# A DeltaNet layer followed by a gated feed-forward block: the same work in another hand-written order

## The chip, the cores and the metric

The kernel runs on one core of a Trainium2 chip, in one launch. The metric is the device time of that launch in microseconds (us). Before the change three runs took 638.85, 640.1 and 642.2 us; their median is 640.1 us.

A core has five engines, each with an instruction queue of its own that it works through strictly in order: PE (TensorE, matrix products), DVE (VectorE), ACT (ScalarE), POOL (GpSimd) and SP (SyncE, which only issues transfers). An instruction whose inputs are not there stops its engine's queue until they come. Transfers (DMAs) are issued here from SP's and ACT's queues, and seven at the start from POOL's.

## The reference

```python
def _attn_ref(q, k, v, beta):               # (4, 8, 768, 48), beta (4, 8, 768)
    k_n = k / (np.linalg.norm(k, axis=-1, keepdims=True) + 1e-06)
    state = np.zeros((B, H, D, D))
    for t in range(S):
        kt, vt, bt = (k_n[:, :, t], v[:, :, t], beta[:, :, t, None])
        y[:, :, t] = np.einsum('bhd,bhde->bhe', q[:, :, t], state)
        v_old = np.einsum('bhde,bhd->bhe', state, kt)
        state = state + bt[:, :, :, None] * np.einsum('bhd,bhe->bhde', kt, vt - v_old)
    return y

def _moe_ref(x, w_in, w_out):               # x (3072, 384), w_in (384, 2048), w_out (2048, 384)
    h = x @ w_in
    g = h * np.cos(h)
    return g @ w_out
# x = the attention's y, transposed to (batch, time, heads * head_dim)
```

All data are float32.

## The kernel before, in words

**The attention** is worked in 24 units n of 32 time steps. Each unit holds all four batches and eight heads. For each unit: `turn` and `turn_out` transpose keys and queries (from unit 6 on, `blocks` loads and DVE transposes do this); `gram` multiplies them on PE, `gram_keys` and `gram_queries` scale and mask the products on DVE. The triangular matrix of a unit must be inverted. For units 0 and 1 this is done by repeated doubling: `double(n, level, half)` on PE (L759) and its `double_copy` (ACT), `double_turn` and `double_add` (DVE), six levels in a chain. From unit 2 on it is done for pairs m = (2m, 2m+1) column by column on POOL: `gram_put` writes the matrices to DRAM, `gram_get` reads them back in another layout, `inv(m, 0..6)` (L879 and L886; `inv(1, 0)` on DVE) eliminates, `put` writes the result, `get` reads it back for one unit. `eye` fills the start value.

Then comes the **recurrence**, which runs from unit to unit: `state(n)` (PE, L930) multiplies by the state, `right(n)` (DVE, L947) forms the right side, `solve(n)` (PE, L1002) multiplies by the inverse, `solve_out(n)` (DVE, L1014) scales, `update(n)` (PE, L1027) and `update_out(n)` (DVE, L1035 or L1037) make the next state. For units 2 and 3 the solve has two halves: `solve_half`, `half_out` (ACT), `between`, `between_out` (DVE), `solve` (L960, L996). Off this chain, `within`, `within_out` (ACT), `features` (PE, L1078) and `features_out` (ACT) make the feed-forward block's input.

**The feed-forward block** takes units in pairs p, 256 tokens. Pair 0 is worked plainly: eight `hidden(0, f)` (PE, L1099, 12 products each), the gate h·cos h by `turns`, `cos` (ACT), `rest`, `gate` (DVE), and eight `out(0, i, k)` (PE, L1297). From pair 1 on both products are Strassen-like: sums of inputs `x_sum` (POOL or DVE, L1188), `layer(p, x)` (PE, L1273), `layer_out` (ACT or DVE), then `left`, `right` sums, `out(p, step, part)` (PE, L1355), `collect` and `store`. `in_sums` and `right` make the sums of the weights. The weights come in 28 pieces by `weights(t)`, are brought to another form by `split(t)` (ACT, L528, L532), `shift(t)` (DVE, L536) and `add(t)` (POOL, L540), and use the same eight tiles as the gates and the squares of the keys (`square`), so that a `weights(t)` or a `square` can wait for the `add` that empties its tile.

**The order** is written out by hand. `Order.add` records 2,199 pieces, each with its dependencies. `Order.LINE` is a list of their numbers; `run` emits the pieces in that order, and each engine then works through its own pieces in that order. Buffers are given out in this order too, first freed first taken. `Order.OTHER` names the pieces that go the other way where there are two: transfers go to ACT's queue if they are named there and to SP's otherwise, sums go to POOL or DVE. `warm(i)` pieces are matmuls on an unused bank (L495) that fill PE's idle time; they emit nothing once the first `out` has been emitted. The last loop of the kernel pins the instructions of each engine in the emitted order.

```python
line = [keys[int(i)] for i in self.LINE.split()]
for key in line:
    emit, deps, makes, uses = self.tasks[key]
    assert deps <= done, key
    for tag, t in makes:
        self.place[t] = free[tag].pop(0)
    emit()
```

Of the kernel before, what the change touches and what calls it, by code (L numbers as in the profile page):

```python
# [59 lines left out]
class Order:  # L60

    OTHER = {
        ('v', 0), ('v', 1), ('gram_put', 2), ('gram_put', 3), ('inv', 1, 0), ('put', 1),
        ('gram_put', 4), ('v', 5), ('gram_get', 2), ('put', 2), ('gram_put', 6), ('v', 8),
        ('v', 9), ('blocks', 9, 0), ('blocks', 9, 1), ('put', 4), ('get', 10), ('v', 11),
        ('blocks', 11, 0), ('blocks', 11, 1), ('gram_put', 11), ('gram_get', 5), ('v', 12),
        ('gram_put', 13), ('gram_get', 6), ('get', 13), ('v', 14), ('blocks', 14, 0), ('v', 15),
        ('blocks', 15, 0), ('blocks', 15, 1), ('v', 16), ('gram_put', 16), ('v', 17), ('k', 18),
        ('v', 18), ('get', 18), ('v', 20), ('gram_put', 21), ('gram_get', 11), ('store', 0, 1),
        ('right', 4, 4), ('left', 1, 1, 0), ('left', 1, 3, 0), ('left', 1, 3, 1),  # L70
        ('store', 1, 0), ('store', 1, 1), ('x_sum', 2, 'd'), ('x_sum', 2, 'n'),
        ('x_sum', 2, 'm'), ('x_sum', 2, 'e'), ('x_sum', 2, 'k'), ('x_sum', 2, 'g'),
        ('x_sum', 2, 'i'), ('x_sum', 2, 'l'), ('x_sum', 2, 'f'), ('x_sum', 2, 'b0'),
        ('left', 2, 4, 1), ('left', 2, 3, 1), ('x_sum', 3, 'd'), ('x_sum', 3, 'n'),
        ('x_sum', 3, 'm'), ('x_sum', 3, 'e'), ('x_sum', 3, 'k'), ('x_sum', 3, 'g'),
        ('x_sum', 3, 'i'), ('x_sum', 3, 'l'), ('x_sum', 3, 'h'), ('x_sum', 3, 'b0'),
        ('left', 3, 4, 1), ('left', 3, 3, 1), ('store', 3, 0), ('store', 3, 1),
        ('x_sum', 4, 'd'), ('x_sum', 4, 'm'), ('x_sum', 4, 'g'), ('x_sum', 4, 'i'),
        ('left', 4, 3, 0), ('left', 4, 3, 1), ('x_sum', 5, 'd'), ('x_sum', 5, 'e'),
        ('x_sum', 5, 'l'), ('x_sum', 5, 'h'), ('x_sum', 5, 'b0'), ('left', 5, 2, 0),  # L80
        ('left', 5, 4, 1), ('left', 5, 3, 0), ('left', 5, 3, 1), ('x_sum', 6, 'd'),
        ('x_sum', 6, 'g'), ('x_sum', 6, 'l'), ('x_sum', 6, 'f'), ('x_sum', 6, 'b0'),
        ('left', 6, 1, 0), ('left', 6, 4, 0), ('store', 6, 0), ('x_sum', 7, 'd'),
        ('x_sum', 7, 'm'), ('x_sum', 7, 'g'), ('x_sum', 7, 'i'), ('x_sum', 7, 'f'),
        ('x_sum', 7, 'h'), ('x_sum', 7, 'b0'), ('left', 7, 4, 0), ('left', 7, 4, 1),
        ('left', 7, 3, 1), ('store', 7, 0), ('x_sum', 8, 'd'), ('x_sum', 8, 'm'),
        ('x_sum', 8, 'e'), ('x_sum', 8, 'k'), ('x_sum', 8, 'g'), ('x_sum', 8, 'l'),
        ('left', 8, 3, 0), ('store', 8, 0), ('store', 8, 1), ('x_sum', 9, 'd'),
        ('x_sum', 9, 'm'), ('x_sum', 9, 'e'), ('x_sum', 9, 'k'), ('x_sum', 9, 'i'),
        ('x_sum', 9, 'l'), ('x_sum', 9, 'b0'), ('left', 9, 1, 0), ('left', 9, 2, 0),  # L90
        ('left', 9, 1, 1), ('left', 9, 3, 0), ('store', 9, 1), ('x_sum', 10, 'k'),
        ('x_sum', 10, 'i'), ('x_sum', 10, 'l'), ('x_sum', 10, 'h'), ('x_sum', 10, 'b0'),
        ('left', 10, 1, 0), ('left', 10, 1, 1), ('left', 10, 4, 1), ('left', 10, 3, 0),
        ('left', 10, 3, 1), ('store', 10, 1), ('x_sum', 11, 'd'), ('x_sum', 11, 'e'),
        ('x_sum', 11, 'k'), ('x_sum', 11, 'g'), ('x_sum', 11, 'f'), ('left', 11, 1, 0),
        ('left', 11, 2, 0), ('left', 11, 1, 1), ('left', 11, 3, 0), ('left', 11, 3, 1),
        ('store', 11, 1), ('store_right', 11), ('weights', 2), ('weights', 3), ('weights', 4),
        ('weights', 9), ('weights', 11), ('weights', 12), ('weights', 13), ('weights', 14),
        ('weights', 15), ('weights', 17), ('weights', 23), ('weights', 24)
# [1849 lines left out]
```

## Time and profile before

| | |
|---|---|
| median of three runs | 640.1 us |
| profiled execution | 642.77 us |
| its span, first to last instruction | 641.0 us |
| granted TensorE clock, mean | 0.98 |
| busy: PE, DVE, POOL, ACT | 612.1, 504.4, 435.1, 297.5 us |
| chain that ended last: PE, DMA, POOL, DVE | 76%, 8%, 5%, 5% |

Busy time is time in which an engine has at least one instruction in it. The chain that ended last is found by going back from the last instruction, each time to what released it. In a row of the order of time, "x24" counts matmul records: a float32 product is two records, a transpose one.

### The profile page before, as it was taken

The page shows a single profiled execution, that of the slowest core. Times are in us where ns is not written, and L with a number is a line of the kernel's source. Part 1 is how long each engine was busy: PE and PEld are TensorE (multiplying, and loading weights), DVE is VectorE, ACT ScalarE, POOL GpSimd, SP SyncE. Part 2 cuts the span into 40 slices and gives each one's busy share as a digit, 9 for nine tenths or more (in the row PEclk, how much of TensorE's full clock was granted, in tenths as well). Part 3 has the DMA queues.
Part 4 walks back from the last instruction along what each step waited for, and adds up shares of the span by engine and source line. Part 5 has one row for each costly group of instructions (what it writes and reads, how often), then busy time and mean ns, then how long its engine had stood idle before and what let it go on. Part 6 is the DMA issues. An engine that isn't in the chain of part 4 may idle for free.

```text
span 641.0 us, 24058 instructions
## 1 busy us (share of the span) xinstructions
PE 612.1 (95%) x10096; PEld 571.4 (89%) x10096; DVE 504.4 (79%) x1051; ACT 297.5 (46%) x533; POOL 435.1 (68%) x791
## 2 busy tenths in 40 slices
PE   6978788999999999999999999999999999999997
PEld 4857777788799998999999999999999999999997
DVE  5876736999999897788878788978878676757872
ACT  3546535645543543543743553643544443635440
POOL 4428877788888888786886786888884881212231
PEclk8897979999999999999999999999999999999999
DMA  9876656655354645446234445333225011000001
GB/s 187 218 169 174 136 130 134 148 87 83 72 87 74 103 74 96 69 67 111 42 52 87 75 79 91 54 45 70 45 35 101 18 31 23 20 3 15 13 20 30
DMA packets 215844, 50.75 MB, mean 79 GB/s; under 512 B 207384, under 2 KB 210744, under 8 KB 215736
## 3 DMA queue, kind: packets, MB, share of 16 engines
q1 hardware_dynamic: 161132, 32.34, 27.8%
q10 hardware_dynamic: 54300, 16.33, 12.1%
q8 instruction: 79, 1.29, 0.8%
q0 software_dynamic: 304, 0.54, 0.4%
q14 instruction: 29, 0.24, 0.1%
HBM read 38.95 MB, written 10.22 MB: 77 GB/s over the span
## 4 chain that ended last, share of the span: by engine, by line
PE 76%; DMA 8%; POOL 5%; DVE 5%; issue 2%; SPq 2%; ACT 1%; ACTq 1%; DVEq 0%; POOLq 0%
PE p_out L1355 30%; PE p_h L1273 28%; PE p_kq L930 3%; PE p_s L1027 3%; POOL part L879 2%; POOL z L886 2%; PE p_u L1002 2%; PE p_kq L1057 2%; PE p_g L675 2%; PE p_h L1099 2%; DMA qp<-in_q_dram 2%; PE p_h L1355 2%; DMA kp<-in_k_dram 2%; PE p_z L1078 1%; DMA w_sum<-z_dr 1%
## 5 line engine op out<-in xcount | busy, mean ns | idle before, releaser
L879 POOL TENSOR_TENSOR part<-z,gb 128x126 f32<-128x126 f32 (+23 forms) x321 | 141.6, 441 | 44.1 <-DMA gb<-g_dr 17.5
L886 POOL TENSOR_TENSOR z<-z,part 128x126 f32<-128x126 f32 (+23 forms) x321 | 142.8, 445 | 25.2
L1355 PE MATMUL p_out<-w_out,g_ffn 128*128 128x192 f32 x672 | 121.0, 329 | 0.0
L1355 PEld LDWEIGHTS p_out<-w_out,g_ffn 128*128 128x128 f32 x672 | 107.9, 190 | 1.0
L1152 ACT ACTIVATE turns<-turns,halfpi 128x512 f32<-128x512 f32 x96 | 68.0, 718 | 83.2 <-DVE turns L1143 71.6
L1273 PE MATMUL p_h<-x_sum,w_in 128*128 128x128 f32 x704 | 92.3, 278 | 0.0
L1355 PE MATMUL p_out<-w_sum,g_ffn 128*128 128x192 f32 x496 | 88.7, 328 | 0.0
L1273 PEld LDWEIGHTS p_h<-x_sum,w_in 128*128 128x128 f32 x704 | 85.6, 191 | 1.9
L1136 ACT ACTIVATE turns<-g_ffn,quarter_turn 128x512 int32<-128x512 f32 x77 | 55.0, 719 | 66.3 <-DVE g_ffn L1155 35.4
L1355 PEld LDWEIGHTS p_out<-w_sum,g_ffn 128*128 128x128 f32 x496 | 79.6, 190 | 0.6
L1290 DVE TENSOR_TENSOR g_ffn<-g_ffn,p_h 128x512 f32<-128x512 f32 x88 | 59.5, 679 | 14.7 <-PE p_h L1273 13.7
L1155 DVE TENSOR_TENSOR g_ffn<-turns,g_ffn 128x512 f32<-128x512 f32 x77 | 61.7, 810 | 11.7 <-ACT turns L1152 11.6
L1143 DVE SCALAR_TENSOR_TENSOR turns<-g_ffn,turns 128x512 f32<-128x512 f32 x77 | 57.1, 750 | 8.2 <-ACT turns L1136 8.1
L1273 PE MATMUL p_h<-x_sum,in_sum 128*128 128x128 f32 x440 | 58.9, 278 | 0.8 <-POOL x_sum L1188 0.8
L1273 PEld LDWEIGHTS p_h<-x_sum,in_sum 128*128 128x128 f32 x440 | 54.3, 191 | 2.2 <-POOL x_sum L1188 1.0
L1070 ACT COPY y<-p_kq 32x384 f32<-32x384 f32 x96 | 45.1, 470 | 19.0 <-PE p_kq L1057 8.1
L1407 DVE SCALAR_TENSOR_TENSOR o<-p_out,o 128x192 f32<-128x192 f32 x74 | 25.1, 351 | 29.7 <-PE p_out L1355 29.5
L1273 PE MATMUL p_h<-x_ffn,w_in 128*128 128x128 f32 x352 | 46.6, 277 | 1.0 <-ACT p_h L1285 1.0
L1273 PEld LDWEIGHTS p_h<-x_ffn,w_in 128*128 128x128 f32 x352 | 43.0, 192 | 1.6 <-ACT p_h L1285 1.3
L574 POOL TENSOR_TENSOR knrm<-ksum,halves 128x16 f32<-128x16 f32 (+1 forms) x14 | 37.1, 2647 | 10.1 <-DVE ksum L562 9.5
L1371 POOL TENSOR_TENSOR g_ffn<-g_ffn 128x512 f32<-128x512 f32 x15 | 19.1, 1271 | 30.5 <-DVE g_ffn L1155 26.6
L1285 ACT COPY p_h<-p_h 128x512 f32<-128x512 f32 x44 | 25.3, 575 | 28.5 <-PE p_h L1273 20.4
(168 smaller groups left out, 1051.7 us busy)
## 6 DMA issues: line engine op xcount, KB each, us to landing
g_ffn<-in_moe_w_in_dram SPq DMA_DIRECT2D x7, 512.0 KB, 7.8
g_ffn<-in_moe_w_out_dram SPq DMA_DIRECT2D x9, 384.0 KB
kp<-in_k_dram SPq DMA_DIRECT2D x136, 24.0 KB, 2.5
gb<-g_dr SPq DMA_DIRECT2D x12, 256.0 KB, 3.9
g_ffn<-in_moe_w_out_dram ACTq DMA_DIRECT2D x7, 384.0 KB
g_ffn<-in_moe_w_in_dram ACTq DMA_DIRECT2D x5, 512.0 KB, 5.9
vp<-in_v_dram ACTq DMA_DIRECT2D x52, 48.0 KB, 2.7
zt<-z_dr SPq DMA_DIRECT2D x68, 32.0 KB, 2.7
```

The lines of the kernel that those rows point to most:

```text
L574: nc.gpsimd.tensor_tensor(out=scales[m][2][:, part], in0=sums[m, part.start][:, 0:n], in1=halves[:, 0:n], op=ALU.pow,)
L879: eng.tensor_tensor(out=part, in0=z[:, 0:rows, j, None].to_broadcast(shape), in1=a[:, j, None, j + 1 :].to_broadcast(shape), op=ALU.mult,)
L886: eng.tensor_tensor(out=behind, in0=behind, in1=part, op=ALU.subtract)
L1070: nc.scalar.copy(by_parity(y[quarter(b)]), p_kq[quarter(b ^ 1), :, b % 2])
L1136: nc.scalar.activation(turns[p, f], hidden_of(p, f), AF.Identity, bias=quarter_turn, scale=TURN)
L1143: nc.vector.scalar_tensor_tensor(out=r, in0=hidden_of(p, f), scalar=TURN, in1=t, op0=ALU.mult, op1=ALU.subtract,)
L1152: nc.scalar.activation(r, r, AF.Sin, bias=halfpi, scale=2.0 * math.pi)
L1155: nc.vector.tensor_tensor(out=place(p, f), in0=step_of(rests.pop((p, f)), f), in1=step_of(hidden_of(p, f), f), op=ALU.mult,)
L1273: nc.tensor.matmul(p_h[:, e], in_block(*w)[:, e], x_of(p, b), start=new and e == 0, stop=True, skip_group_check=True,)
L1285: nc.scalar.copy(to, part_of(p, one))
L1290: nc.vector.tensor_tensor(out=part_of(p, to), in0=part_of(p, one), in1=part_of(p, two), op=op)
L1355: nc.tensor.matmul(p_o, left(p, part, a)[:, e % 4], right(e, b), start=(e == 0), stop=(e == FT // 2 - 1), skip_group_check=True,)
```

## The change

The computation is the same, piece by piece. Two tables are replaced: `OTHER` and the first 1,100 places of `LINE` (1,073 pieces stand at another place; by the change's own count 781 were moved). The other 1,099 places are the same. No `x_sum`, `left`, `right`, `in_sums` or `inv` goes to another engine. Of the transfers, 33 pieces (82 DMAs) go from ACT's queue to SP's, and 18 pieces (60 DMAs) from SP's to ACT's.

```diff
     OTHER = {
-        ('v', 0), ('v', 1), ('gram_put', 2), ('gram_put', 3), ('inv', 1, 0), ('put', 1),
-        ('gram_put', 4), ('v', 5), ('gram_get', 2), ('put', 2), ('gram_put', 6), ('v', 8),
...
+        ('k', 3), ('gram_put', 3), ('inv', 1, 0), ('put', 1), ('get', 4), ('blocks', 6, 0),
+        ('blocks', 6, 1), ('v', 7), ('k', 8), ('blocks', 9, 0), ('k', 11), ('blocks', 11, 1),
...
     LINE = """
-0 8 9 27 10 11 28 29 2087 1 2 5 31 139 3 4 7 32 83 84 33 85 30 34 142 2091 2095 36 88 38 86 143 41
...
+0 27 28 8 9 10 11 1 31 29 2 3 83 2087 84 5 32 139 26 30 140 33 2091 2095 34 85 142 86 4 88 36 35 12
...
```

In names, PE's order from solve(0) to solve(2):

```
before: solve(0) double(1,4,1) update(0) within(0) double(1,5,1) double(1,3,0) state(1)
        double(1,4,0) features(0) double(1,5,0) gram(4) hidden(0,0) solve(1) update(1) within(1)
        turn(5) gram(5) warm hidden(0,2) features(1) state(2) hidden(0,4) solve_half(2) between(2)
        hidden(0,6) solve(2)
after:  double(1,3,0) double(1,4,1) solve(0) warm double(1,4,0) update(0) within(0) warm warm
        double(1,5,1) features(0) state(1) hidden(0,0) gram(4) double(1,5,0) solve(1) warm
        update(1) within(1) turn(5) gram(5) hidden(0,2) features(1) state(2) hidden(0,4)
        hidden(0,6) solve_half(2) out(0,0,0) between(2) solve(2)
```

From solve(2) to features(3) PE's order is the same but for two `warm` pieces, which go; out(0,0,0) stood behind state(4) and gram(7) before.

Other places that the prediction speaks of, as they stand on their queues after the change:

```
DVE:  ... double_turn(1,3,0) shift(7) solve_out(0) shift(9) sum(2,0) update_out(0) inv(1,0) shift(5)
      double_add(1,5,1) scale(2,0) right(1) in_sums(0) gram_keys(4) gram_queries(4)
      double_add(1,5,0) solve_out(1) ... turn_out(6) update_out(2) right(3) ...
ACT:  ... turn_out(4) square(2,0) split(7) split(8) double_copy(1,4,0) double_copy(1,4,1) split(9)
      within_out(0) ... half_out(2) cos(0,4) split(18) split(17) blocks(6,0) cos(0,6) ...
      half_out(3) turns(0,8) k(8) weights(23) cos(0,8) cos(0,10) split(22) split(23) split(19)
      within_out(3) turns(0,14) features_out(3) ...
POOL: ... add(2) add(0) add(6) add(1) add(4) add(7) add(3) add(9) norms(2,0) inv(1,1) ...
      norms(3,0) add(13) add(16) inv(2,0) ...
SP:   ... gram_put(5) gram_put(4) get(2) gram_get(2) ... gram_put(10) put(4) gram_put(11) get(8) ...
      put(5) gram_put(13) get(10) ... put(6) get(12) ...
```

More of the change, by code (lines that the diff above doesn't have):

```diff
@@ L69 @@
[L69 to L74, printed above, removed]
@@ L93 @@
[L93 to L98, printed above, removed]
@@ L100 @@
+        ('store', 10, 1), ('x_sum', 11, 'd'), ('x_sum', 11, 'e'), ('x_sum', 11, 'k'),
+        ('x_sum', 11, 'g'), ('x_sum', 11, 'f'), ('left', 11, 1, 0), ('left', 11, 2, 0),
+        ('left', 11, 1, 1), ('left', 11, 3, 0), ('left', 11, 3, 1), ('store', 11, 1),
+        ('store_right', 11), ('weights', 1), ('weights', 4), ('weights', 5), ('weights', 9),
+        ('weights', 14), ('weights', 16), ('weights', 18), ('weights', 21), ('weights', 22),
+        ('weights', 23)
     }
```

50 lines of the change are left out of this document (27 added, 23 removed), and 96 rows, old and new, of the table LINE.

## The prediction

> **What bounds the kernel now.** I read the page first, then the busy time of each engine by stretch, then the chain that ended last, and last the order of time on single engines. The page gives one number:
>
> ```profile
> span 641.0 us, 24058 instructions
> ```
>
> The profiled execution took 642.77 us, so 1.8 us lie outside its span. The median of the runs is 640.1, 2.67 below this execution; I make the sum against 642.77 and take 2.67 off at the end. The stretches (columns: width, then busy time of PE, PE's weight loads, DVE, ACT, POOL, then the granted clock, the DMA share and GB/s):
>
> ```profile
> 0.00:20.00 20.00, 13.61 (x204) 10.98 (x206) 12.80 (x43) 5.53 (x11) 10.32 (x18) 0.78 0.89 178
> 20.00:40.00 20.00, 18.00 (x360) 15.20 (x356) 17.23 (x50) 13.70 (x28) 5.58 (x4) 0.96 0.78 223
> 40.00:60.00 20.00, 14.98 (x387) 13.13 (x388) 15.16 (x47) 11.12 (x23) 13.37 (x19) 0.89 0.70 168
> 60.00:80.00 20.00, 16.43 (x307) 15.20 (x306) 13.86 (x27) 10.86 (x21) 16.86 (x20) 0.94 0.66 138
> 80.00:100.00 20.00, 16.91 (x396) 15.66 (x397) 9.40 (x23) 8.54 (x17) 14.65 (x36) 0.83 0.62 137
> 100.00:120.00 20.00, 16.93 (x585) 14.58 (x578) 14.61 (x29) 10.22 (x20) 17.55 (x38) 1.00 0.59 123
> 120.00:240.00 120.00, 118.91 (x2045) 104.38 (x2044) 112.70 (x231) 59.15 (x105) 102.52 (x184) 1.00 0.53 89
> 310.00:620.00 310.00, 310.00 (x4560) 299.55 (x4559) 243.38 (x477) 146.84 (x254) 192.60 (x355) 1.00 0.26 46
> ```
>
> From 120 us on PE is the bound: 118.91 of 120, then 310.00 of 310, at full clock. The work is unchanged, so an order can only change PE's idle and slow time, and that lies in the first six rows: 120 − 96.86 = 23.1 us idle, with clocks of 0.78 to 0.96 in five of them. Every microsecond of PE work that is pulled into this front ends the kernel a microsecond earlier, as long as the stretch behind stays full. There DVE is nearly full too: 112.70 of 120.
>
> What holds the front up is the recurrence. The chain of waits shows it between 58 and 84 us (start, length, what):
>
> ```profile
> 58.78 4.68 PE p_h L1099 x24
> 63.47 1.09 PE p_u L1002 x32
> ...
> 67.94 1.04 PE p_t L642 x8
> ...
> 71.03 0.43 DVE g L696
> 71.48 0.40 SPq L833
> ...
> 71.98 1.30 SPq L902
> ...
> 75.95 6.62 DMA w_sum<-z_dr
> ...
> 82.71 1.29 PE p_w L960 x48
> ```
>
> hidden(0,0) (L1099) stands ahead of solve(1) (L1002) on PE; behind that come turn(5), gram_keys(5), and on SP's queue gram_put(5), ahead of get(2). get(2)'s data land at 82.57, and solve_half(2) waits for them. PE in order of time there (the bracket is the idle time before the row):
>
> ```profile
> 75.63 2.94 PE L1099 MATMUL p_h<-x_ffn,w_in 128*128 128x128 f32 x24
> 79.18 0.24 PE L960 MATMUL p_w<-rhs,w_sum 32*32 32x48 f32 x2 [0.61 <-DMA w_sum<-z_dr]
> 81.66 0.24 PE L960 MATMUL p_w<-rhs,w_sum 32*32 32x48 f32 x2 [2.24 <-DMA w_sum<-z_dr]
> 82.71 1.54 PE L960 MATMUL p_w<-rhs,w_sum 32*32 32x48 f32 x60 [0.81 <-DMA w_sum<-z_dr]
> 84.87 1.50 PE L960 MATMUL p_v<-g_ffn,in_sum 32*32 32x48 f32 x64 [0.62 <-ACT g_ffn L972]
> 86.30 4.62 PE L1099 MATMUL p_h<-x_ffn,w_in 128*128 128x128 f32 x24
> ```
>
> PE waits 3.66 us for the landing, and hidden(0,6), which follows, takes 4.62 instead of the 2.94 of its sister: the clock fell in the wait.
>
> **The change, part by part.** No instruction is added. One of the 15 filling matmul pairs (L495) goes, since out(0,0,0) now stands ahead of it. The first 1,100 of 2,199 places of the order are rearranged; the second half is word for word the same. 33 pieces (82 DMAs) go from ACT's queue to SP's, 18 pieces (60 DMAs) the other way; SP issues 537 instead of 515.
>
> (1) *The doubling stage, up to solve(1).* The two series of doublings are now interleaved from the start, beta_home and the v loads leave the way, and the last doubling of unit 1 needs less behind it. DVE paces this stage, and its own idle time is the room:
>
> ```profile
> 46.71 0.42 DVE L779 TENSOR_TENSOR in_sum<-in_sum,p_h 128x256 f32<-128x256 f32 x1 [1.66 <-PE p_h L759]
> 48.25 1.02 DVE L1014 TENSOR_TENSOR u<-p_u,bz 128x384 f32<-128x384 f32 x2 [0.76 <-PE p_u L1002]
> 52.59 0.42 DVE L779 TENSOR_TENSOR w_sum<-w_sum,p_h 128x256 f32<-128x256 f32 x1 [1.26 <-PE p_h L759]
> 64.58 1.02 DVE L1014 TENSOR_TENSOR u<-p_u,bz 128x384 f32<-128x384 f32 x2 [3.35 <-PE p_u L1002]
> ```
>
> Together 7.0 us, the upper bound. The lower bound is zero or a loss: on DVE shift(7) and shift(9) now stand ahead of solve_out(0) and update_out(0). They wait for ACT's split(7) and split(9), ACT for square(2,0), and this for a buffer that POOL's add(1) frees, behind add(6) and shift(6). All of state, right and solve(1) is queued behind them; I bound a jam there by the same 3.35 us as a loss. The value I take is the row nearest to it, the 3.35 us before solve_out(1): solve(1) waited for hidden(0,0), and the new order brings hidden(0,0) forward ahead of gram(4) and the last doubling. solve(1), turn(5), gram_put(5), get(2) and solve_half(2) all come 3.35 us earlier by it.
>
> (2) *Filling the wait.* hidden(0,6) goes ahead of solve_half(2): 2.94 us into a wait of 3.66, which moves with (1). Behind solve_half(2) out(0,0,0) takes its place, before between(2). Its price:
>
> ```profile
> 98.95 0.60 PE L495 MATMUL p_out<-o 128*128 128x256 f32 x2
> ...
> 100.94 0.60 PE L495 MATMUL p_out<-o 128*128 128x256 f32 x2
> ...
> 118.33 5.43 PE L1297 MATMUL p_out<-w_out,g_ffn 128*128 128x384 f32 x16
> ```
>
> The 16 matmul records are two output pieces, so one is 2.72. The way from between(2) to solve(2) thus carries 2.72 instead of 4.62: −1.9. If the clock is at half there, 2.72 becomes 5.43 and this is +0.8; as the wait left over is about 0.7 us, I take −1.9. The two fillers, 1.2 us, leave the way to state(4). And the 2.72 of out(0,0,0) is no longer to be done at 118: −2.72. The last of its weights, add(13), now stands right ahead of it, on POOL behind norms(3,0); if that is late, PE stands at out(0,0,0) with between(2) and solve(2) behind it. I let it wait for nothing, and leave its lateness to C below.
>
> Here the clock has to be weighed. Its fall shows twice:
>
> ```profile
> 58.00:64.00 6.00, 6.00 (x100) 0.62 0.66 183
> ...
> 83.00:86.00 3.00, 2.38 (x115) 0.50 0.70 172
> ```
>
> Before the first of these PE's longest wait in 20 us is this:
>
> ```profile
> 36.32 1.96 PE L759 MATMUL p_h<-w_sum 64*64 64x128 f32 x32 [1.67 <-DVE w_sum L775]
> ```
>
> So by the rows the clock falls after thin activity, without one long wait, and I leave hidden(0,0) its 4.68 us in the new order too. [...]
>
> (3) *Queues.* ACT loses loads that blocked it and gets others. Of its own, before (first row DMA issue, second what stood behind it):
>
> ```profile
> 108.18 3.66 ACTq L398 DMA_DIRECT2D vp<-in_v_dram x4
> 112.24 1.91 ACT L1070 COPY y<-p_kq 32x384 f32<-32x384 f32 x4 [4.01 <-DMA vp<-in_v_dram]
> ```
>
> That is v(5) ahead of within_out(3). In the new order v(5) is SP's, but k(8), with eight DMAs, comes to ACT ahead of cos(0,8), and weights(23) with split(23) stand ahead of within_out(3) and features_out(3), for which all of layer 1 waits. On DVE turn_out(6) now stands ahead of update_out(2), and waits for blocks(6,0), which ACT issues behind split(17). Eight DMAs instead of four at 0.92 us each (3.66/4) cost ACT 3.7 us more at most; nothing where ACT idles anyway. I take the middle, +1.9, bounds 0 and +3.7; DVE's turn_out(6) is inside this.
>
> (4) *The stretch behind.* To keep a gain, DVE must do its 112.70 us of 120:240 in less: it idles only 7.3 there. DVE also enters earlier, by what (1) saves it. I take +2.5 given back to DVE's pace, between 0 and 7.3.
>
> Sum: −3.35 −1.9 −1.2 −2.72 +1.9 +2.5 = −4.8. 642.77 − 4.8 = 638.0 for an execution like the profiled one, and less 2.67: **635.3 us**. With the terms at their good ends (−7.0, 0, 0) it is 640.1 − 12.8 = 627.3; with (1) at +3.35, (2) at −3.1 (1.2 and 2.72 less the 0.8 of a slow clock), (3) at +3.7, (4) at +7.3, it is +11.2: 651.3.
>
> **The rivals.** A: *the gain is real in front and given back behind.* For it speaks DVE's 112.70 of 120, POOL's 102.52, and that lengths are not fixed. One shape on POOL (min, median, max in ns):
>
> ```profile
> L1188 POOL TENSOR_TENSOR x_sum<-x_sum,x_ffn x22: 445/458/967, 117.7 to 586.3; 128x128 f32<-128x128 f32 x22
> ```
>
> The same addition takes 0.45 or 0.97 us, depending on what runs beside it, so an order worked out with lengths from a trace meets other lengths. If DVE's work grows by 6.5% (7.3/112.7) its idle time is gone. [...] Against A: DVE idles 22 us in 60:120 (its three rows sum to 37.87 of 60), so it can enter 120 with more done. Under A the −9.2 of (1) and (2) keeps 1 to 2: about 639, no change. That the new order does not do what it says, because the landings come otherwise, ends in the same place.
>
> B: *SP becomes the bound (slower).* SP runs its queue in order, and in the new order get(8) stands behind gram_put(11), get(10) behind gram_put(13), each of which waits for DVE; get(12) is just behind put(6). What such a piece waits, before (total us, times, longest), and what a late get does to PE:
>
> ```profile
> SPq L833 <- DVE tt L815: 16.1, 4, 7.2
> ...
> 178.68 0.67 PE L1002 MATMUL p_u<-rhs,zt 64*64 64x48 f32 x30 [0.34 <-DMA zt<-z_dr]
> ```
>
> Mean 4.0 us. solve(6) already waited 0.34 for its landing, so nearly all of a late get goes to PE, which has no other work in its order there. Three of them cost 12.1: 635.3 + 12.1 = 647.4. It decides from 2.7 us a piece (8.0/3: 643.3, slower than the bound below). Against it: the two gram_keys stand ten and eleven places ahead of the get in the order.
>
> C: *a jam in front, as in (1) or at add(13).* With (1) at its +3.35 instead of −3.35, and (3) at +3.7, the time is 635.3 + 6.7 + 1.8 = 643.8.
>
> **How the numbers follow.** A measurement of this kernel can tell 0.5%, 3.2 us, from no change: faster is below 636.9, slower above 643.3. The forecast, gain in front kept in part, 0.51, with its own range 630 to 637; A 0.26 (637 to 643); B 0.13; C 0.10. So faster 0.51, same 0.26, slower 0.23. The range reaches from 629, with a few per cent below, to 647, with some 7% above, B's far half.
>
> **What would show it.** (1) right: the changed profile has solve(1)'s L1002 before 61 us on PE; wrong: at 63 or later, with DVE idle before L1014 or L1037 on an L528/L536 piece. (2) right: no wait over 1.5 us before the first L960, an L1297 of 2.7 us between the two L960 groups, and clock 1.0 there. (3): the last transposes L1078 of unit 3 at 110 to 113 us instead of 116. (4) and A: PE under 118 of 120 in the stretch behind, with DVE the releaser. B: PE idle before L1002 on zt<-z_dr by 2 us or more. The forecast is wrong if the front is not at least 4 us shorter, or if PE idles more than 4 us between 120 and 310.

## The result, and the profile after

| | before | after |
|---|---|---|
| median (four runs each, same chip) | 640.28 us | 655.44 us |
| range | 638.85 to 642.2 | 654.62 to 656.91 |
| ratio, 95% interval | | 1.0237 [1.0204, 1.027] |
| profiled execution, span | 642.77, 641.0 us | 655.8, 654.0 us |
| busy: PE, DVE, POOL, ACT | 612.1, 504.4, 435.1, 297.5 | 615.7, 512.5, 433.2, 299.0 |

The change makes the kernel 2.4% slower; the forecast was 635.3 us, 0.7% faster. The span grows by 13.0 us: PE is busy 3.6 us longer (615.7 − 612.1, for the same work) and idles 9.4 us longer (38.3 against 28.9).

The stretches of the kernel after, with the columns of the prediction's table:

```profile
0.00:120.00 120.00, 97.58 (x2231) 82.43 (x2232) 89.79 (x219) 64.20 (x125) 78.92 (x135) 0.97 0.72 163
120.00:240.00 120.00, 113.32 (x1914) 101.07 (x1913) 108.56 (x219) 54.20 (x96) 95.05 (x174) 0.97 0.49 85
240.00:310.00 70.00, 66.70 (x1126) 63.02 (x1125) 54.65 (x113) 29.46 (x52) 55.17 (x109) 1.00 0.42 69
310.00:620.00 310.00, 307.77 (x4634) 296.68 (x4633) 240.87 (x475) 143.61 (x248) 194.74 (x369) 0.99 0.28 50
```

PE's busy time in the first 120 us is 97.58 against the 96.86 of before, at a granted clock of 0.97 instead of 0.90. Behind it PE idles 6.7 us, then 3.3, then 2.2, where before it idled 1.1 in 120:240 and nothing in 310:620. PE has done the same pieces in both orders when it comes to solve(4), and again at update(13), just behind the rearranged part. These two places are a better ruler than equal times. The stretch between them, before, after and in links2 (a run told of below):

```profile
129.13:325.48 196.35, 194.29 (x3373) 178.61 (x3372) 175.16 (x360) 93.79 (x166) 165.83 (x317) 1.00 0.48 79
```

```profile
125.27:338.48 213.21, 202.16 (x3373) 185.57 (x3372) 180.38 (x365) 94.68 (x167) 164.26 (x313) 0.97 0.45 75
```

```profile
125.04:329.92 204.88, 197.02 (x3372) 179.57 (x3371) 180.35 (x365) 94.30 (x165) 171.35 (x325) 1.00 0.47 78
```

In this pair of profiles the new order is thus 3.9 us ahead at solve(4) (125.27 against 129.13) and loses 16.9 us from there to update(13): 9.0 in PE's idle time (11.05 against 2.06) and 7.9 in slower work at a lower clock (0.97 against 1.00).

PE's order of time shows the rows of the prediction's signs and the longest waits behind 120 us (start, length, what; the bracket is the idle time before the row and what ended it):

```profile
54.82 2.92 PE L1097 MATMUL p_h<-x_ffn,w_in 128*128 128x128 f32 x24 [0.55 <-ACT x_ffn L1084]
59.70 1.14 PE L1000 MATMUL p_u<-rhs,w_sum 64*64 64x48 f32 x32 [0.56 <-DVE w_sum L777]
...
80.49 0.84 PE L958 MATMUL p_w<-rhs,w_sum 32*32 32x48 f32 x58 [1.08 <-DMA w_sum<-z_dr]
81.25 2.85 PE L1295 MATMUL p_out<-w_out,g_ffn 128*128 128x384 f32 x8
...
97.65 1.19 PE L958 MATMUL p_w<-rhs,w_sum 32*32 32x48 f32 x64 [1.37 <-ACT x_ffn L1084]
99.46 1.50 PE L958 MATMUL p_v<-g_ffn,in_sum 32*32 32x48 f32 x64 [0.62 <-ACT g_ffn L970]
100.90 3.70 PE L1097 MATMUL p_h<-x_ffn,w_in 128*128 128x128 f32 x24
...
112.66 0.49 PE L1076 MATMUL p_z<-consts,y 128*128 128x128 f32 x3
...
171.47 5.46 PE L1271 MATMUL p_h<-x_sum,w_in 128*128 128x128 f32 x24 [3.26 <-DVE x_sum L1186]
...
264.21 0.68 PE L1000 MATMUL p_u<-rhs,zt 64*64 64x48 f32 x30 [0.62 <-DMA zt<-z_dr]
...
324.47 2.05 PE L1271 MATMUL p_h<-x_sum,w_in 128*128 128x128 f32 x8 [2.23 <-ACT g_ffn L1285]
```

solve(1) starts at 59.70, out(0,0,0) takes 2.85, features(3) is at 112.66: each as the forecast asked. Then come two things that it did not have: hidden(0,12) at 100.90 takes 3.70 instead of 2.94, and single long waits of PE at 171 and 324 us.

What stands behind the late ones is in POOL's order of time: the first step of inv(4) and of inv(7) (128x31 rows), and the sum between.

```profile
181.34 0.24 POOL L877 TENSOR_TENSOR part<-z,gb 128x31 f32<-128x31 f32 x1 [4.82 <-DMA vp<-in_v_dram]
...
314.91 0.46 POOL L1186 TENSOR_TENSOR x_sum<-x_sum,x_ffn 128x128 f32<-128x128 f32 x1 [10.76 <-DVE x_sum L1186]
...
319.46 0.24 POOL L877 TENSOR_TENSOR part<-z,gb 128x31 f32<-128x31 f32 x1 [1.90 <-DMA gb<-g_dr]
```

inv(4) starts at 181.3 (before at 175.8), inv(7) at 319.5 (304.1). For inv(4) the releaser named is not the cause, since inv(4) reads no v: what came last is eye(4), its start value, on ACT:

```profile
180.66 0.61 ACT L865 COPY z<-consts 128x512 f32<-128x512 f32 x1
```

For inv(7) the chain of waits has it (SPq is a transfer being issued from SP's queue):

```profile
301.02 0.23 POOL z L884
301.27 3.24 DMA z_dr<-z
304.59 0.31 SPq L908
...
306.43 0.44 SPq L415
...
308.51 0.49 SPq L396
...
313.52 4.36 DMA gb<-g_dr
317.95 1.75 DMA zt<-z_dr
319.70 0.70 ACT turns L1150
...
324.47 2.05 PE p_h L1271 x8
```

inv(6) ends at 301.25. put(6) stands on SP's queue waiting for it, and behind put(6) stand get(12) (L908), blocks(17,0) (L415), k(18) (L396) and only then gram_get(7), whose data start at 313.5. The pause from inv(6) to inv(7) is thus 18.2 us; before it was 10.1.

### The profile page after: what moved, and what is told of

It is laid out like the page before. It is cut to its first block, busy times and chain, and to the rows that moved or that the text cites. A ratio compares the mean times of both kernels' runs of the same rounds, so it can differ in the third digit from the quotient of the medians.

```text
span 654.0 us, 24064 instructions
## 1 busy us (share of the span) xinstructions
PE 615.7 (94%) x10094; PEld 573.0 (88%) x10094; DVE 512.5 (78%) x1051; ACT 299.0 (46%) x533; POOL 433.2 (66%) x791
## 4 chain that ended last, share of the span: by engine, by line
PE 68%; DVE 9%; DMA 6%; POOL 6%; SPq 4%; ACT 3%; issue 2%; ACTq 0%; DVEq 0%; POOLq 0%
PE p_h L1271 25%; PE p_out L1353 25%; POOL part L877 3%; PE p_kq L928 3%; POOL z L884 3%; DMA gb<-g_dr 2%; PE p_s L1025 2%; PE p_kq L1055 2%; PE p_g L673 2%; SPq L396 2%; PE p_u L1000 2%; PE p_h L1353 2%; PE p_h L757 2%; PE p_out L1295 1%; DMA kp<-in_k_dram 1%
## 5 line engine op out<-in xcount | busy, mean ns | idle before, releaser
L877 POOL TENSOR_TENSOR part<-z,gb 128x126 f32<-128x126 f32 (+23 forms) x321 | 141.3, 440 | 55.8 <-DMA gb<-g_dr 26.0
L884 POOL TENSOR_TENSOR z<-z,part 128x126 f32<-128x126 f32 (+23 forms) x321 | 140.6, 438 | 25.2
L1353 PE MATMUL p_out<-w_out,g_ffn 128*128 128x192 f32 x672 | 123.9, 332 | 0.8 <-DVE o L1405 0.7
L1353 PEld LDWEIGHTS p_out<-w_out,g_ffn 128*128 128x128 f32 x672 | 109.4, 193 | 2.4 <-issue 1.3
L1271 PE MATMUL p_h<-x_sum,w_in 128*128 128x128 f32 x704 | 96.1, 285 | 6.7 <-ACT g_ffn L1285 3.4
L1271 PEld LDWEIGHTS p_h<-x_sum,w_in 128*128 128x128 f32 x704 | 89.1, 198 | 8.7 <-ACT turns L1134 3.7
L1141 DVE SCALAR_TENSOR_TENSOR turns<-g_ffn,turns 128x512 f32<-128x512 f32 x77 | 58.8, 770 | 11.7 <-ACT turns L1134 11.5
L572 POOL TENSOR_TENSOR knrm<-ksum,halves 128x16 f32<-128x16 f32 (+1 forms) x14 | 36.7, 2625 | 21.2 <-DVE ksum L560 18.9
```

Source lines behind the costliest of these rows:

```text
L572: nc.gpsimd.tensor_tensor(out=scales[m][2][:, part], in0=sums[m, part.start][:, 0:n], in1=halves[:, 0:n], op=ALU.pow,)
L877: eng.tensor_tensor(out=part, in0=z[:, 0:rows, j, None].to_broadcast(shape), in1=a[:, j, None, j + 1 :].to_broadcast(shape), op=ALU.mult,)
L884: eng.tensor_tensor(out=behind, in0=behind, in1=part, op=ALU.subtract)
L1141: nc.vector.scalar_tensor_tensor(out=r, in0=hidden_of(p, f), scalar=TURN, in1=t, op0=ALU.mult, op1=ALU.subtract,)
L1271: nc.tensor.matmul(p_h[:, e], in_block(*w)[:, e], x_of(p, b), start=new and e == 0, stop=True, skip_group_check=True,)
L1353: nc.tensor.matmul(p_o, left(p, part, a)[:, e % 4], right(e, b), start=(e == 0), stop=(e == FT // 2 - 1), skip_group_check=True,)
```

## The experiments

Six kernels put the two orders together in parts, twelve move single pieces. Each ratio is to runs of the kernel before on the same chip, so medians from different chips are compared by their ratios. "Inverse starts" below are the first instruction of inv(m) in the profiled executions. In all of these profiles the span ends 286 to 288.5 us after inv(8) begins, as the second half of the order is the same in all; inv(8) therefore marks how late a kernel is by then.

**Which part of the order.** The first n places from the new order, the rest from the old one; `OTHER` likewise, piece by piece.

```diff
+new = after[:440]                  # front_only; 560: cut560; 660: cut660
+LINE = new + [k for k in before if k not in new]
+old = before[:440]                 # back_only
+LINE = old + [k for k in after if k not in old]
```

> The first 440 pieces of the line (what runs up to about 124 us) as after the change, all others in the order and on the queues of before. Theory O (the loss is made by the new order behind 120 us, and the gain in front is real): PE's lost time up to 120 us is 39.3 us as after instead of 44.4 before, nothing is lost behind, 640.3 - 5.1 = 635.2 us. Rival D (the lead cannot be kept, since DVE is at its pace from 120 to 240 us): PE waits some 4 to 5 us more between 120 and 240 than before, 639 to 641 us.

> The first 440 pieces as before the change, all others in the order and on the queues of after. Theory O: the loss behind 120 us, 13.0 + 5.1 = 18 us of PE's waits and slow clock, comes in full on top of before: 658 us (655 to 660). Rival D: the new order behind suffers only because PE comes early to work that DVE has not done; with the old front the wait of 3.26 us at 171 us and the slow clock behind it (2.7 us) are gone: 652 us or less.

> The first 560 pieces (up to about 160 us) as after, the rest as before; with 440 pieces it was 643.9 us, with 660 pieces 650.5 us. If the loss arises at the links between inv(3) and inv(4), gram(9), put(3), get(6), gram_get(4) and eye(4), all of which stand behind place 560 in the new order (theory C): 641 to 646 us. If it arises by the order of DVE's work between 124 and 160 us (rival D): 648 us or more.

> The first 660 pieces (what runs up to about 185 us, the start of inv(4) among them) as after, all others in the order and on the queues of before. Theory C: inv(4) starts at 181 us as after, 8 us later than in a run with the old order (172.9), and this is carried to the end: 647 us (646 to 649). Rival P (PE's lost time is what counts: 39.1 us at 180 us against 35.1 in a run with the old order): 644 us or less.

| | median | ratio | inv(8) starts |
|---|---|---|---|
| front_only (440) | 643.87 | 1.0077 [1.0049, 1.0104] | 355.1 |
| cut560 | 646.86 | 1.012 [1.0078, 1.0163] | 355.8 |
| cut660 | 650.47 | 1.0195 [1.0137, 1.0254] | 362.2 |
| after (1,100) | 655.44 | 1.0237 [1.0204, 1.027] | 368.0 |
| back_only | 654.16 | 1.0237 [1.0199, 1.0275] | 363.6 |

So the front, on which the whole forecast rested, brings no gain at all: alone it costs 0.8%. The back alone costs as much as all of the change; the parts do not add up.

**Which half of the tables.** The new order with the old queues, and the other way round.

```diff
-LINE = before; OTHER = before
+LINE = after;  OTHER = before      # order_only
+LINE = before; OTHER = after       # queues_only
```

> The new order with the queues of before (each load, store, put and get on SP or ACT as before the change). Theory Q (the queues carry the loss: by 300 us SP has 19 us more of issues ahead and ACT 20 us less, and put, get and gram_get stand in SP's line behind loads): 646 us or less. Theory C (the order of the chain's links on PE, DVE and ACT carries it): 651 us or more.

> The old order with the new queues. Theory Q: at least half of the loss, 647 us or more. Theory C: 639 to 644 us.

order_only took 681.44 us (1.0675 [1.0625, 1.0725]), queues_only 658.48 (1.031 [1.027, 1.0349]). Each half alone is worse than both, so neither is the culprit by itself: the places of the transfers in the order are fitted to the queue on which they stand. How a misfit costs is seen in queues_only, on ACT's queue:

```profile
143.76 4.08 ACTq L398 DMA_DIRECT2D kp<-in_k_dram  x8
147.93 0.57 ACT L1285 COPY p_h<-p_h 128x512 f32<-128x512 f32 x1 [8.69 <-DMA qp<-in_q_dram]
```

and on PE, where the next product waits for that copy to empty its bank:

```profile
148.56 1.86 PE L1273 MATMUL p_h<-x_sum,in_sum 128*128 128x128 f32 x7 [7.32 <-ACT p_h L1285]
```

Loads named for ACT stand ahead of a copy of a feed-forward product; the copy idles 8.69 us behind them, and PE 7.32.

**The waits of PE, one by one.** In the new order the pieces whose lateness the profile names behind 160 us were moved out of each other's way.

```diff
 DVE:  ... x_sum(2,e)
+      x_sum(2,k) x_sum(2,g)        # forward: wait at 171 us
 ACT:  ... layer_out(5,1)
+      v(14) get(13)                # back: wait at 305 us
 POOL: ... x_sum(5,i)
+      x_sum(5,g)                   # forward, ahead of inv(7,0)
 SP:   ... 
+      gram_put(15) put(6)          # gram_put(15) from ACT's queue
```

> After, with the waits of PE at 171, 304 and 324 us taken at what released them: x_sum k and g of unit 2 ahead of two sums of weights on DVE, x_sum g of unit 5 ahead of the inverse on POOL, gram_put(15) from ACT to SP ahead of put(6), v(14) and get(13) on ACT behind layer_out(5,1). Theory P (time is lost where PE waits, with the clock fall behind): 3.3 + 2.7 at 171 us, 1.6 at 304 and 2.2 + 3.3 at 324 come back, 13 us: 642 us (641 to 646). Rival C (the inverses of POOL, late by 14 us at inv(7), set when the solves come; solve(14) has 2.5 us of slack only): no more than 2.5 us, 653 us or more.

It took 655.31 us (1.0252 [1.0221, 1.0284]): nothing gained. The wait at 171 went from 3.26 to 1.35, but PE's wait at solve(10) grew from 1.58 (0.96 + 0.62) to 3.70 us:

```profile
260.81 0.28 PE L1000 MATMUL p_u<-rhs,zt 64*64 64x48 f32 x2 [2.38 <-DMA zt<-z_dr]
262.41 1.10 PE L1000 MATMUL p_u<-rhs,zt 64*64 64x48 f32 x30 [1.32 <-DMA zt<-z_dr]
```

The last data of the inverse come only 1.8 us earlier than in after (262.41 instead of 264.21), and PE, now ahead, waits for them. Taking away single waits of PE brought no time back. The counterpart puts one such wait into the old order:

```diff
 before, DVE: ... right(6)
+      x_sum(2,g)                   # from 7 places ahead of right(6)
```

> Before the change, one local wait of PE added: x_sum g of unit 2 behind right(6) on DVE, at about 171.8 instead of 167 us, so that layer(2,1) waits some 2 us where it waited for nothing. Rival P: the wait and a clock fall behind it show at the end: 642 to 645 us. Theory C: PE has room before it meets the inverses at the next solve, and DVE catches up: 640 to 641 us.

640.51 us (1.0013 [0.9975, 1.0051]), though PE waits 1.81 us ahead of a product at 169.8. A late sum alone is absorbed where the chain of inverses is on time: inv(4) starts at 173.1 there. (The wait is smaller than the 3.26 us of after, and the product behind it takes 2.92 us, not 5.46.)

**The chain of inverses.** One inverse can start when its gram_get has landed, its eye is there and POOL comes to it; POOL's norms and sums stand behind it in order. First the link of inv(7):

```diff
 after, SP:   ... put(6)
+      gram_get(7)                  # ahead of get(12): chain
 before, SP and POOL: ... k(19)
+      gram_get(7) inv(7,0)         # behind k(19), on POOL behind x_sum(5,g): late_link
```

> After, with gram_get(7) ahead of get(12) on SP, so that inv(7) starts at about 310 instead of 319 us, and nothing else moved. Rival C: the inverse was what set the end behind 300 us: at least 5 us of the 13 come back, 650 us or less. Theory P: PE's waits at 171 and 304 us are untouched and only what x_sum g of unit 5 waited for behind inv(7,0) goes (2.2 us, with 3.3 us of slow clock if the wait falls below the one at 304): 650 to 655 us; if ACT alone was what held layer(5,1), 655 us.

> Before the change, one link late: gram_get(7) and inv(7,0) behind k(19) on SP, so that gram_get(7) goes out at 307.6 instead of 295.4 us and inv(7) starts at about 312.5 instead of 303.8 us. Theory C: solve(14) had 3.3 us of slack (get(14) at 344.5, its first part some 2.9 us later, solve(14) at 350.6), so 5 us of the 8.7 show: 645 us (643 to 648). Rival P: the chain has room and PE fills the time with other work: 640 us.

chain took 656.04 us (1.026 [1.022, 1.0299]); inv(7) starts at 319.7, no earlier. POOL stood meanwhile at x_sum(5,k) (10.76 us in after, above, and 11.99 here), which stands ahead of inv(7) and waits for DVE's x_sum(5,e): one of two obstacles had been taken away. late_link does the harm to the old order, alone, and takes 645.61 us (1.008 [1.005, 1.0109]); inv(7) starts at 308.1 instead of the 302.2 of late_sum. Its profile shows the way to PE, on POOL, DVE and PE:

```profile
333.31 2.91 POOL L574 TENSOR_TENSOR knrm<-ksum,halves 128x16 f32<-128x16 f32 x1
```

```profile
336.26 0.32 DVE L603 TENSOR_TENSOR knrm<-knrm,tiny 128x16 f32<-128x16 f32 x1 [6.27 <-POOL knrm L574]
```

```profile
338.69 2.08 PE L1273 MATMUL p_h<-x_ffn,w_in 128*128 128x128 f32 x8 [3.81 <-DVE g_ffn L1290]
```

norms(8,0) stands behind inv(7) on POOL; DVE's scale(8,0) waits for it 6.27 us at the head of its queue, layer_out stands behind scale on DVE, and PE's next product, whose bank layer_out empties, waits 3.81. In this run a late inverse reaches PE not through solve but through POOL's and DVE's in-order queues; from update(13) to the end of the span it takes 322.7 us, late_sum 315.6. scale also leads to the next gram, gram_put, gram_get and so to the next inverse, so lateness is handed on.

**Repairing the links.** The next five kernels move links forward in the new order: the first two many at once, the others one corner of the chain or both.

```diff
 chain2:  gram, gram_keys, gram_queries, gram_put of pairs 5 to 7 and gram_get, eye of
+         pairs 4 to 7 some places forward; gram_put(15) from ACT's queue to SP's;
+         inv(4,0) behind norms(6,0); inv(5,0) behind get(8); inv(7,0) behind x_sum(5,n)
 both2:
+         chain2 and stalls
 fix_a:   gram_keys(9) behind gram(9) (DVE's own order stays as it is); x_sum(2,k) x_sum(2,g)
+         behind x_sum(2,e); gram_get(4) ahead of get(6); eye(4) ahead of layer_out(2,3); inv(4,0) behind norms(6,0)
 fix_b:
+         gram_get(7) ahead of get(12); x_sum(5,e) behind gate(4,(0,0,1));
+         v(14) get(13) behind layer_out(5,1)
 fix_ab:
+         fix_a and fix_b
```

> After, with the links between the inverses earlier, so that each inv(m) starts sooner behind inv(m-1): gram_get(4) to (7) ahead of the get of the same inverse, eye(4), eye(5), eye(6), eye(7) earlier on ACT, gram_keys/gram_queries 10, 11, 13, 15 straight behind their gram on DVE, gram(11), (13), (15) a few places earlier on PE, gram_put(11), (13), (15) ahead of put(4), (5), (6) on SP, inv(4,0), (5,0), (7,0) earlier on POOL. Theory C (two bounds in series: the inverses' chain, met by PE at solve(10)): inv(7) starts at 304 to 310 instead of 319 us and PE's waits at solve(10) are gone; what is left are PE's local waits at 171, 304 and 324 us: 648 to 653 us. Rival P (PE's local waits alone): 655 us, unchanged.

> The earlier links of the run before and the edits at PE's waits of 171, 304 and 324 us (as in the run that had these alone, which gave nothing) in one. Theory C: each of the two hides the other, so that only both give the time back: 12 us or more, 643 us or less. Rival L (the front's lead has nowhere to go and the new order behind is slow for another reason, such as DVE's pace): 648 us or more.

> After, with the corner between inv(3) and inv(4) mended, where the start of the inverse falls from 2 us ahead of a run with the old order to 8 us behind it: gram_keys(9) straight behind gram(9) and x_sum k and g of unit 2 straight behind x_sum e on DVE, gram_get(4) ahead of get(6) on SP, eye(4) ahead of layer_out(2,3) on ACT, inv(4,0) behind norms(6,0) on POOL. Theory C (the order behind is paced by the loop inverse - norms on POOL - scale on DVE - gram - inverse, so the end comes as much later as an inverse starts later): inv(4) starts at about 176 instead of 181 us and the end comes 5 us earlier, 650 us (648 to 652). Rival E (a delay taken out in one place comes back at the next, as in the runs before): 654 us or more.

> After, with the corner between inv(6) and inv(7) mended, where the start of the inverse falls from 8.5 to 17 us behind: gram_get(7) ahead of get(12) on SP, x_sum e of unit 5 behind gate(4,(0,0,1)) on DVE so that POOL's x_sum k, i and g of unit 5 don't wait 10.8 us in front of inv(7), v(14) and get(13) on ACT behind layer_out(5,1). Theory C: inv(7) starts at about 311 instead of 319 us and the end comes 7 to 8 us earlier, 647 us (646 to 650). Rival E: 654 us or more.

> Both corners mended. Theory C: the two add, 642 to 645 us. Rival E: 652 us or more.

| | median | ratio | inv(4) | inv(7) | inv(8) |
|---|---|---|---|---|---|
| after | 655.44 | 1.0237 [1.0204, 1.027] | 181.3 | 319.5 | 368.0 |
| chain2 | 656.68 | 1.0256 [1.0188, 1.0324] | 179.9 | 316.5 | 373.5 |
| both2 | 656.25 | 1.0255 [1.0197, 1.0313] | 177.8 | 309.0 | 367.9 |
| fix_a | 652.62 | 1.0226 [1.0173, 1.0279] | 180.8 | 320.1 | 367.5 |
| fix_b | 655.95 | 1.0254 [1.0197, 1.0311] | 180.8 | 308.3 | 366.0 |
| fix_ab | 649.82 | 1.0192 [1.0124, 1.026] | 182.7 | 311.4 | 366.9 |

None of the five separates from after by its interval; the profiled execution of fix_ab, from which its starts are, took 656.5 us, its other three 647.9 to 650.1. chain2 and both2 made a jam of their own: inv(5,0) was put ahead of POOL's sums of pair 3 and held them while it waited for its matrices, in both2 so:

```profile
220.37 0.24 POOL L877 TENSOR_TENSOR part<-z,gb 128x31 f32<-128x31 f32 x1 [7.56 <-DMA gb<-g_dr]
```

with PE waiting 6.38 us at 225. fix_b brings inv(7) forward by 11.2 us and inv(8) by 2.0 only. POOL, early with inv(7), stands in front of norms(8,0) and waits for DVE:

```profile
338.92 3.29 POOL L572 TENSOR_TENSOR knrm<-ksum,halves 128x16 f32<-128x16 f32 x1 [4.33 <-DVE ksum L560]
```

scale(8,0), which needs norms(8,0), done at 342.2, comes on DVE at 347.1 only (348.6 in after). So DVE's own work is late there, with the inverse on time; why was not followed further. fix_a's execution was late from the front on: inv(3) starts at 136.1 in it and at 132.2 in after. From inv(3) to inv(4) it takes 44.7 us instead of 49.2 (39.1 before), so this link did get shorter. gram(9) stays late: gram_put(9) is issued at 166.1 us in after and at 162.7 in late_sum.

So all links were moved together, gram(9) too:

```diff
 links_all, in LINE after, for pairs 4 to 7:
+  gram_keys, gram_queries straight behind their gram; gram(9) behind out(0,1,2), gram(11)
+  behind out(1,4,0), gram(13), gram(15) behind features_out(9), (11); each gram_put behind
+  its gram_keys; put(3) gram_get(4) behind gram_put(9); gram_get(5) behind gram_put(11);
+  gram_get(6), (7) ahead of get(10), (12); eye(4) behind layer_out(2,5); eye(5) behind
+  layer_out(2,34); inv(4,0) behind left(1,1,0); x_sum(2,k) x_sum(2,g) x_sum(5,e) as above;
+  put(4) ahead of gram_keys(10); v(14) get(13) behind layer_out(5,1); eye(7) some places
+  forward, blocks(12,1) back
 links2:
-  put(4), eye(5), v(14), get(13) of these
+  gram_get(5) behind put(4); v(14) behind right(12); get(13) behind cos(4,(1,1,1))
```

> After, with every link from one inverse to the next as early as its own inputs allow: gram_keys and gram_queries 8 to 11, 13 and 15 straight behind their gram, gram(9), (11), (13), (15) some places earlier on PE, put(3) and put(4) and gram_get(4) to (7) ahead of what stood before them on SP, eye(4), (5), (7) earlier, x_sum k, g of unit 2 and e of unit 5 earlier on DVE, v(14), get(13) and blocks(12,1) later on ACT; no inverse is moved ahead of POOL's sums of units 3 and 5 this time. Theory C: inv(4) at 172 to 176 us, inv(7) at 308 us or before, 644 us or less. Rival E (what is gained at one link is lost at another): 650 us or more.

> links_all without its two own mishaps: eye(5) back where after has it (it had waited 10.4 us for put(4) and kept ACT's work of unit 2), put(4) and gram_get(5) behind gram_put(11) again, v(14) right behind right(12), get(13) behind cos(4,(1,1,1)), blocks(12,1) behind rest(2,(0,1,0)). Theory C: PE's wait at 218 us (3.1 us and 2.2 us of slow clock) and the waits at 325 to 328 us (1.6 us) go, inv(7) starts at about 302 us, and the time is 645 us (642 to 648). Rival E: 650 us or more.

links_all took 652.12 us (1.0206 [1.0166, 1.0246]). inv(4) now starts at 172.4, but eye(5), moved too far forward, held ACT while the z tile that it fills was still being written out, and PE with it (ACT's row, then PE's):

```profile
213.67 0.62 ACT L865 COPY z<-consts 128x512 f32<-128x512 f32 x1 [10.42 <-DMA z_dr<-z]
```

```profile
218.11 2.21 PE L1353 MATMUL p_out<-w_out,g_ffn 128*128 128x192 f32 x8 [3.13 <-DVE o L1405]
```

links2, without that, took 649.45 us (1.0164 [1.0132, 1.0195]), an interval that lies below that of after: the links together are worth about 0.7% (1.0237 − 1.0164). inv(4) starts at 173.3, inv(7) at 303.6, both as in the old order, inv(8) at 358.4 (368.0 after, 354.2 before). Its stretches behind 120:

```profile
120.00:240.00 120.00, 113.75 (x1930) 100.53 (x1929) 111.01 (x222) 54.84 (x97) 101.32 (x185) 1.00 0.51 86
240.00:310.00 70.00, 68.38 (x1166) 64.19 (x1165) 56.12 (x115) 29.39 (x52) 57.51 (x116) 1.00 0.46 78
```

240:310 has most of its loss back (68.38; 66.70 after, 69.03 before). 120:240 does not: 113.75, with DVE now at 111.01.

**The fillers.** The last run takes links2 and gives PE back the two silent filling products:

```diff
 links2, PE:
-      solve_half(2) out(0,0,0) between(2) ... 
+      ... out(0,0,0) out(0,0,1) ...     # out(0,0,0) back to its old place
+      warm(14) state(3) ... features(2) warm(15)
```

> links2 with out(0,0,0) back straight ahead of out(0,0,1), so that the two filling products warm(14) and warm(15) are emitted, ahead of state(3) and of solve_half(3). Theory W (the fillers' loss lets the clock fall): the clock stays at 1.0 from 96 to 104 us and hidden(0,12) takes 2.94 instead of 4.21 us; in exchange the wait around solve_half(2), which out(0,0,0) had filled, is open again, and hidden(0,6) or solve_half(2) is slow at 78 to 87 us; at the end 647 to 651 us, as links2 or 2 us less. Rival N (the clock falls there whatever stands between the waits): hidden(0,12) at 3.7 us or more.

651.73 us (1.0163 [1.0107, 1.0219]). The stretch from 96 to 104 us in after, in fillers and in the old front (late_sum); the granted clock is the third number from the end:

```profile
96.00:104.00 8.00, 6.01 (x152) 5.52 (x151) 5.79 (x13) 2.64 (x6) 7.29 (x14) 0.79 0.51 72
```

```profile
96.00:104.00 8.00, 5.53 (x151) 4.47 (x150) 5.12 (x12) 4.85 (x10) 6.98 (x16) 1.00 0.57 101
```

```profile
96.00:104.00 8.00, 6.89 (x241) 6.08 (x233) 3.83 (x8) 5.54 (x11) 7.29 (x14) 1.00 0.74 129
```

With the fillers the clock holds (1.00 in 96:104 and in 104:108) and hidden(0,12) takes 2.94 again. The time is no better. In that profile another product of the same kind, hidden(0,8), is the slow one:

```profile
86.26 1.49 PE L1097 MATMUL p_h<-x_ffn,w_in 128*128 128x128 f32 x11
90.01 3.14 PE L1097 MATMUL p_h<-x_ffn,w_in 128*128 128x128 f32 x13 [2.26 <-issue]
```

Its 24 records take 6.89 us from first to last instead of 2.94, with a pause of 2.26 for which the profile shows no cause. Pauses of this kind, 0.28 to 1.14 us long, stand in 7 of the 13 profiles of the new front, always behind the third record of hidden(0,8) or the tenth of hidden(0,10), and in none of the four of the old front between solve(2) and solve(3). So it is not this execution alone; what PE waits for in them no profile says.

No version that was run beats the kernel before.

## Why the prediction was wrong, point by point

**The front's gain, terms (1) and (2), −9.2 us: not there at its end.** All three signs of the front came true (solve(1) at 59.70, no wait over 1.5 us ahead of solve_half(2) and 2.85 for out(0,0,0) at clock 1.00, features(3) at 112.66). But the signs compared one execution of the new front with one of the old, and that one was a bad one. The table has the three other profiles of the old front, and after and the twelve runs that keep its first 440 places as "the new front" (fillers, which moves out(0,0,0), is not among them):

| start of | before | late_sum | late_link | back_only | after | all 13 of the new front |
|---|---|---|---|---|---|---|
| solve(1) | 63.4 | 61.9 | 60.6 | 59.9 | 59.7 | 59.0 to 63.8 |
| solve(2) | 90.8 | 86.5 | 86.8 | 85.7 | 85.6 | 83.5 to 89.0 |
| solve(3) | 107.5 | 103.2 | 103.5 | 102.4 | 104.5 | 104.3 to 109.6 |
| features(3) | 116.0 | 112.0 | 111.6 | 110.6 | 112.7 | 112.7 to 117.4 |
| solve(4) | 129.1 | 126.4 | 125.0 | 123.6 | 125.3 | 124.4 to 130.4 |

That solve(1) comes 3.7 us earlier than in the profile before, near the 3.35 of (1), is luck: it is 0.2 to 2.2 us against the other three. The 4.68 us of hidden(0,0), on which (1) put its 3.35, was 2.94 in each of them, as here in late_sum:

```profile
58.99 2.94 PE L1099 MATMUL p_h<-x_ffn,w_in 128*128 128x128 f32 x24
...
96.58 0.60 PE L495 MATMUL p_out<-o 128*128 128x256 f32 x2
97.51 1.21 PE L960 MATMUL p_w<-rhs,w_sum 32*32 32x48 f32 x64 [0.33 <-ACT x_ffn L1086]
99.50 0.88 PE L960 MATMUL p_v<-g_ffn,in_sum 32*32 32x48 f32 x64 [0.78 <-ACT g_ffn L972]
100.32 2.94 PE L1099 MATMUL p_h<-x_ffn,w_in 128*128 128x128 f32 x24
```

At solve(2) the new front is 1.7 us earlier (medians 84.9 of 13 profiles, 86.6 of 4) and has done out(0,0,0) besides: by the medians, filling the wait, the core of (2), works. It is lost right behind. From solve(2) to solve(3) the old front takes 16.7 us in each of its four profiles, the new one 18.9 to 23.7, though PE's pieces there are the same but for the fillers. At solve(4), where PE has done the same pieces in both, the new front is 0.9 us later (126.6 against 125.7). The step that failed first is the choice to read a fallen clock as a property of the order ("I leave hidden(0,0) its 4.68 us in the new order too"). hidden(0,0) took 2.92 us in after, at a granted clock of 1.00 in 54:58. That thin activity made the clock fall in the profile before (4.68 us, 0.62 in 58:64) was the author's reading of one execution; what made it fall there no run shows.

**"The two fillers, 1.2 us, leave the way": the wrong sign.** They do leave, as the first `out` now comes at 81 us and silences the two that stand after it. But the rows of late_sum show what the filler at 96.58 did: it keeps PE at work ahead of the 0.33 us wait. Without it after waits 1.37 and 0.62 us around solve_half(3), and hidden(0,12) takes 3.70 to 5.18 us in all 13 profiles of the new front, 2.94 in all 4 of the old and in fillers. Where the fillers run the clock holds (1.00 in 96:104 in before, late_sum, back_only and fillers); but in each of these profiles out(0,0,0) also stands at its old place, so the fillers were not tested by themselves. The slow product is only a part of what solve(2) to solve(3) loses: PE also waits 0.35 to 1.75 us for ACT ahead of state(3), where the old front waits for nothing, and the pauses told of above fall there. How much of front_only's 0.8% each makes is not shown; fillers did not become faster.

**(3), queues +1.9:** not to be separated. features(3) is at 112.66 as said, but three profiles of the old front have it at 110.6 to 112.0, and queues_only and order_only show that order and queues have no separate price.

**(4), +2.5 given back to DVE's pace, at most 7.3: the size and the mechanism failed.** In the pair of profiles the terms (1) to (3), together −7.3, came to −3.9 at solve(4); what (4) put at +2.5 came to +16.9 from there to update(13) (213.2 against 196.4). PE's idle time in 120:310 is 10.0 us (6.7 + 3.3), where the old order has 2.1, and the prediction's last sign (more than 4 us) fired. DVE is not fuller than before, 108.56 of 120. What failed is the reading of the stretch by busy shares: full engines alone do not keep it together. One thing that does is the chain of inverses, each link of which goes through SP, POOL, ACT and DVE in order, and the new order puts other pieces ahead of several links. What is shown of its price is that one late link costs the old order 0.8% (late_link) and that mended links give the new one 0.7 of its 2.4% back (links2). That the rest of the loss comes from it too is not shown. The page's group of the inverse has it in one row (count | busy, mean ns | idle before, longest releaser), for before, after and links2:

```profile
L879 POOL TENSOR_TENSOR part<-z,gb 128x126 f32<-128x126 f32 (+23 forms) x321 | 141.6, 441 | 44.1 <-DMA gb<-g_dr 17.5
```

```profile
L877 POOL TENSOR_TENSOR part<-z,gb 128x126 f32<-128x126 f32 (+23 forms) x321 | 141.3, 440 | 55.8 <-DMA gb<-g_dr 26.0
```

```profile
L877 POOL TENSOR_TENSOR part<-z,gb 128x126 f32<-128x126 f32 (+23 forms) x321 | 139.2, 434 | 44.5 <-DMA gb<-g_dr 20.8
```

The work of the inverses is the same; POOL's idle time before them grows from 44.1 to 55.8 us, and repairing the links takes it back to 44.5. But the row does not follow the time: links2 is 1.6% slower than before at 44.5, and front_only 0.8% slower at 43.8. The prediction had the row of DVE's sums and the share of POOL, not this one.

**Rival A** (given back behind) had its place right and its cause wrong. **Rival B** (SP) named a right neighbour: put(6) and get(12), which it listed, do stand ahead of gram_get(7). But it let the late transfer hit PE at solve, and its sign is not there in after (0.96 and 0.62 us at solve(10)); what was late was the matrix going in, not the inverse coming out. **C** did not happen: solve(1) was early.

**What stays open.** links2 is still 1.6% slower than before. Up to inv(7) its inverses start as early as in the old order, and yet it takes 204.9 us from solve(4) to update(13), where before takes 196.4: PE idles 7.9 us instead of 2.1 and is busy 2.7 longer. Its waits there, none over 1.8 us, are for ACT, DVE and transfers, and were not tied to one cause. 0.8% goes with the first 440 places alone; whether that adds to the rest is not known, since front and back do not add.

## What to carry to other kernels

Before a forecast rests on a slow stretch of one profiled execution, ask whether the work there could have run at full clock with the same instructions (here hidden(0,0): 4.68 us in one profile of the old front, 2.94 in three); a gain that is only the loss of a clock fall is not a gain of the order. In a kernel with in-order queues (in queues_only a copy stood 8.69 us behind loads on ACT's), list the longest chain that crosses them (here gram, gram_put, gram_get, inverse, norms, scale, gram) and ask of a new order what it puts ahead of each link on each queue. To see where an order gains and loses, compare the times at which an engine has done the same set of pieces (here solve(4) and update(13) on PE), over several profiles; equal windows, busy shares and the idle time before the chain's own instructions did not show it here. A filler that stops by itself at some first use is part of the order: when that use moves forward, look what the silent fillers had covered.

## What the runs showed of the hardware

The clock fell behind waits of different length. In after it did behind 1.37 and 0.62 us (hidden(0,12) 3.70 instead of 2.94; granted clock 0.79 in 96:104), behind 3.26 us at 171 (24 records in 5.46 us, against 2.94 for 24 records of the same shape elsewhere; granted clock 0.50) and behind 2.23 us at 324 (8 records in 2.05; granted clock 0.50); behind 1.62 us at 305 it did not (8 records in 1.16; granted clock 1.00):

```profile
305.14 1.16 PE L1271 MATMUL p_h<-x_sum,in_sum 128*128 128x128 f32 x8 [1.62 <-ACT p_h L1283]
```

And hidden(0,0) took 4.68 us in one of four profiles of the same old front (granted clock 0.62 in 58:64) and 2.94 in three.

One addition had two lengths, with other work of DVE beside it. POOL's x_sum<-x_sum,x_ffn (128x128, L1188 in before) took 0.97 us at 442.79, beside DVE's g_ffn<-g_ffn,g_ffn (L1371, 0.68 us from 442.76), and 0.45 us at 577.55, beside DVE's g_ffn<-g_ffn,p_h (L1290, 0.69 us from 577.47). Why is not shown.
